# A tuned attention and gMLP kernel: two more Strassen blocks for tokens 512 to 1023, four softmax denominators moved off the matmul engine, and a shorter list of first loads

## The chip, the cores and the metric

The kernel runs on one core of one Trainium2 chip. The metric is the device time of one execution in microseconds (us). The kernel before takes 1762.01 us (median of three executions, 1760.74 to 1764.03).

Names of engines: PE is the matmul engine, PEld its weight loads, DVE the vector engine, ACT the scalar engine, POOL the general engine, SP the engine whose queue issues nearly all DMA here. PSUM is the memory that PE writes its results to. A line such as L507 is a line of the program. The change shifts the program by a few lines, so the same statement is L507 before and L509 after.

## The reference, cut to what matters

```
def A(x, k_cache, v_cache, wq, wo):              # 32 heads of 128, 2048 queries, 2048 keys
    q = (x @ wq) by heads
    p = softmax(q @ k_cache^T * 128 ** -0.5)
    return (p @ v_cache, heads joined) @ wo
def B(x, w_in, w_sp, b_sp, w_out):               # S = 2048 tokens, F = 3584, Fh = 1792
    z = gelu(x @ w_in)
    z1, z2 = z[..., :Fh], layernorm(z[..., Fh:])
    g = einsum('ts,bsf->btf', w_sp, z2) + b_sp   # the spatial gate: mixes tokens
    return (z1 * g) @ w_out                      # the last projection
sa, ca, ga, sb, cb, gb = silu(c) @ w_mod         # six vectors of 1024
x = x + ga * A(layernorm(x) * (1 + ca) + sa, ...)
x = x + gb * B(layernorm(x) * (1 + cb) + sb, ...)
```

All inputs and the output are bf16; x is 2048 tokens by 1024.

## The kernel before

The program is about 1,800 lines. Four of its parts matter here.

**The start.** The first eight tiles of 128 tokens, the vector c and the first pieces of w_mod are loaded on one queue, in this order.

```
for ti in range(8):
    nc.sync.dma_start(xg[ti // 2][:, ti % 2], x_dram[:, ti, :])
    if ti == 1:
        nc.sync.dma_start(c_sb[:], c.rearrange("o (kc p) -> (o kc) p", p=P))
load_wm(2)
load_wm(3)
...                                                             # cut
```

**The attention.** It works through 64 "halves" (one head, 1024 queries each), numbered i = 0 to 63. The softmax denominator of half i - 1 is made during half i, in one of two ways. In halves up to 8 it is made on PE by `finish_here`, eight matmuls with one output column each. Later halves store the partial sums, read them back transposed by a DMA, and reduce them on DVE in `finish_den`. "Halves 5 to 8" are those values of i.

```
def finish_here(i, new_ps=qb_ps):
    dps = new_ps("dps", [P, 8])
    for c_ in range(8):
        nc.tensor.matmul(dps[:, c_:c_ + 1], state[i]["pacc"][:, c_ * P:(c_ + 1) * P],
                         ones_bf[:, 0:1], start=True, stop=True)
    ...                                                         # cut: reciprocal, spread
def finish_den(i):
    ...                                                         # cut
    nc.vector.tensor_reduce(out=den[:], in_=state[i]["pT"][:], op=ALU.add,
                            axis=mybir.AxisListType.X)
    ...                                                         # cut
# per half i and key block kb, near the end of the loop:
        if i > 0:
            work = ({4: lambda i: jobs.append(lambda tag: finish_here(i, tag)),
                     15: load_rec} if i <= 8 else
                    {3: finish_here, 6: load_rec} if final else
                    {0: store_sums, 3: turn_sums, 10: finish_den, 13: load_rec}).get(kb)
            if work:
                work(i - 1)
        if kb == (6 if i <= 9 else 4) and i > 1:
            normalise(i - 2)
```

**Strassen's products.** Where weights and data allow, a 2x2 block product is done with seven products in place of eight; the sums that this takes run on DVE. A `Block` runs its products 1, 2, 6, 7, 5, 3, 4 and empties PSUM through `snap` and `out`, which on DVE take the matmul engine's result and add a second operand (`plus`).

**The end of the program.** The spatial gate has two stages: tokens 0 to 1023, then 1024 to 2047, seven blocks (p = 0 to 6) each. Between them stands the plain last projection of tokens 0 to 1023, in eight tiles of two halves of 14 matmuls. The second stage needs the spatial weights, scaled and summed on DVE (`scale_w`, `w_sums`), and z2, loaded by DMA and normalised on ACT (`norm_z`). After it comes the projection of tokens 1024 to 2047 as four Strassen blocks.

```
def project(ti, between=()):
    ...                                                         # cut
    for j in range(2):
        for f in range(NF):                                     # NF = 14
            nc.tensor.matmul(bo, z1T[0, f // 2][:, f % 2, ti * P:(ti + 1) * P],
                             wout[f // 2][:, f % 2, sl], ...)
        plus(outt[:, sl], bo, x1rs[ti][:, sl])
        work(5 if ti == 2 else 3)()                             # some tasks on DVE
    nc.sync.dma_start(out_dram[:, ti, :], outt[:])

for ti in range(8):
    if ti == 2:
        tasks += scale_w() + w_sums()
    elif ti == 3:
        load_b(1)
        load_z(1, 0, 0)
        load_z(1, 0, 1)
        load_z(1, 1, 0)
        load_z(1, 1, 1)
        load_z(1, 2, 1)
    elif ti == 6:
        norm_z(1, 0, 0)
        norm_z(1, 0, 1)
        norm_z(1, 1, 1)
    project(ti, last + [weights] if not ti else ())
```

The softmax here doesn't subtract the row's maximum and nothing guards it: scores larger than these inputs give would overflow.

Of the kernel before, what the change touches and what calls it, by code (L numbers as in the profile page):

```python
# [9 lines left out]
BF16 = mybir.dt.bfloat16  # L10
# [6 lines left out]
def kernel(  # L17
# [66 lines left out]
    sums_dram = dram.tile([4, P, 1024], BF16)  # L84
    h1_dram = dram.tile([2, P, D], BF16)
    mod_dram = dram.tile([4, D], FP32)
    h2_dram = dram.tile([S, D], FP16)
    rec_dram = dram.tile([2 * H, 1024], FP32)

# [33 lines left out]
    kts[0] = att.tile([P, S], BF16, name="kT", tag="kT", bufs=2)  # L123
    vs[0] = att.tile([P, NKB, DH], BF16, name="v_sb", tag="v_sb", bufs=2)
    nc.scalar.activation(small.tile([P, 1], FP32, name="warm_e")[:], eps_tile[:], ACT.Exp)
    for ti in range(8):
        nc.sync.dma_start(xg[ti // 2][:, ti % 2], x_dram[:, ti, :])
        if ti == 1:
            nc.sync.dma_start(c_sb[:], c.rearrange("o (kc p) -> (o kc) p", p=P))
    load_wm(2)  # L130
    load_wm(3)
    nc.sync.dma_start(wq_g[0][:, :, 0:256], wq_v[:, :, 0:256])
# [646 lines left out]
    for g, (i, kb) in enumerate(steps):  # L779
# [97 lines left out]
            fills(i, kb)  # L877
        if i > 0:
            work = ({4: lambda i: jobs.append(lambda tag: finish_here(i, tag)),
                     15: load_rec} if i <= 8 else  # L880
                    {3: finish_here, 6: load_rec} if final else
                    {0: store_sums, 3: turn_sums, 10: finish_den, 13: load_rec}).get(kb)
            if work:
                work(i - 1)
        if kb == (6 if i <= 9 else 4) and i > 1:
            normalise(i - 2)

    left.__exit__(None, None, None)
# [14 lines left out]
    def scratch(name, shape, dtype=FP32):  # L903
        return scr.tile(shape, dtype, name=name, tag="k2", bufs=11)
# [6 lines left out]
    def after(n, fn):  # L911

        later.append([n, fn])
# [464 lines left out]
    def w_sums():  # L1378

        t = {}  # L1380

        def one(n, u, s):
            if n != 1 and (n, u) not in t:
                t[n, u] = heap.take(f"w_t{n}", [P, 4, 512], FP16)
            t[1, u] = W[0, 1, u]
            a, b = {3: (W[1, 1, u], t[1, u]), 1: (t[1, u], W[0, 0, u]),
                    2: (W[1, 1, u], t[1, u]), 4: (W[1, 0, u], t.get((2, u)))}[n]
            nc.vector.tensor_sub(out=t[n, u][:, s], in0=a[:, s], in1=b[:, s])
            if n == 4 and u == 1:
                for v in range(2):  # L1390
                    wb.update({(1, v): W[0, 0, v], (2, v): W[1, 0, v], (3, v): W[1, 1, v],
                               (4, v): t[4, v], (5, v): t[1, v], (6, v): t[2, v],
                               (7, v): t[3, v]})
        return [lambda n=n, h=h: one(n, h // 2, slice(2 * (h % 2), 2 * (h % 2) + 2))
                for n in (3, 1, 2, 4) for h in range(4)]
# [39 lines left out]
    def work(n=1):  # L1435
        def go():
            for _ in range(n):
                if tasks:
                    tasks.pop(0)()
        return go  # L1440
# [114 lines left out]
        nc.sync.dma_start(x1rs[ti][:], x1_dram[ti])  # L1555

    def project(ti, between=()):
        if ti + 2 < 8:
            load_x1(ti + 2)
        outt = scratch("outt", [P, D], BF16)  # L1560
        for j in range(2):
            sl = slice(j * 512, (j + 1) * 512)
            bo = bank_ps("bo", [P, 512])[:]
            for f in range(NF):
                nc.tensor.matmul(bo, z1T[0, f // 2][:, f % 2, ti * P:(ti + 1) * P],  # L1565
                                 wout[f // 2][:, f % 2, sl], start=(f == 0),
                                 stop=(f == NF - 1), skip_group_check=True)
                if f == NF - 3 and not j:
                    for fn in between:
                        fn()  # L1570
            plus(outt[:, sl], bo, x1rs[ti][:, sl])
            work(5 if ti == 2 else 3)()
        nc.sync.dma_start(out_dram[:, ti, :], outt[:])


# [3 lines left out]
    def unit():  # L1579
        if not units:  # L1580
            t = heap.take("units", [P, 4, 512], FP16)
            units.extend(t[:, k, :] for k in range(4))
        return units.pop(0)

    ps_, pt_ = {}, {}

    def p_sum(p, n):

        z = z1T[1, p]
        a11, a21, a12, a22 = (z[:, k, i * 512:(i + 1) * 512] for k in range(2) for i in range(2))  # L1590
        t = ps_[p, n] = a21 if n == 3 else unit()
        a, b = {1: (a21, a22), 2: (ps_.get((p, 1)), a11), 3: (a11, a21),
                4: (a12, ps_.get((p, 2)))}[n]
        (nc.vector.tensor_add if n == 1 else nc.vector.tensor_sub)(out=t, in0=a, in1=b)

    def wp_sum(p, n):
# [5 lines left out]
                4: (b21, pt_.get((p, 2)))}[n]  # L1602
        nc.vector.tensor_sub(out=t, in0=a, in1=b)

    outts = {}

    def proj_block(m):
        done = {1: 0, 2: 0}

        def operands(n):  # L1610
            sl, ps = slice(m * P, (m + 1) * P), range(NG)
            hi = slice(512 + m * P, 512 + (m + 1) * P)
            a = {1: (0, sl), 2: (1, sl), 7: (0, hi), 4: (1, hi)}.get(n)
            lhs = ([z1T[1, p][:, a[0], a[1]] for p in ps] if a else
                   [ps_[p, {5: 1, 6: 2, 3: 4}[n]][:, sl] for p in ps])
            b = {1: (0, 0), 2: (1, 0), 3: (1, 1)}.get(n)
            rhs = ([wout[p][:, b[0], b[1] * 512:(b[1] + 1) * 512] for p in ps] if b else
                   [pt_[p, {5: 1, 6: 2, 7: 3, 4: 4}[n]] for p in ps])
            return lhs, rhs

        def snap(ps, which):
            t = scratch("snap", [P, 512])[:]
            ti, s0 = ((8 + m, 0), (12 + m, 0), (12 + m, 512))[which - 1]
            plus(t, ps, x1rs[ti][:, s0:s0 + 512])
            return t

        def out(i, j, ps, other):
            ti, sl = 8 + m + 4 * (i - 1), slice((j - 1) * 512, j * 512)
            if not done[i]:
                outts[ti] = scratch("outt", [P, D], BF16)  # L1630
            plus(outts[ti][:, sl], ps, x1rs[ti][:, sl] if other is None else other)
            done[i] += 1
            if done[i] == 2:
                nc.sync.dma_start(out_dram[:, ti, :], outts[ti][:])

        return Block(operands, snap, out)

    def last_block(f, prev):


        def product(n, bank, cols=slice(0, 512), first=True):
# [16 lines left out]
        product(5, a, first=False)  # L1658
        u = f.snap(a, 3)
        product(7, b)  # L1660
        o11, o15 = scratch("outt", [P, D], BF16), scratch("outt", [P, D], BF16)
        done(15, o15, right_, b, u)
        plus(x, b, x)
        c = single_ps("c")[:]
        product(2, c)
        done(11, o11, left_, c, s)
        product(3, a, first=False)
        done(11, o11, right_, a, x1rs[11][:, right_])
        for c0, c1 in ((0, 256), (256, 384), (384, 512)):
            ps = single_ps("d")[:, 0:c1 - c0]  # L1670
            product(4, ps, slice(c0, c1))
            done(15, o15, slice(c0, c1), ps, x[:, c0:c1])

    gates = [[gate_block(c, p) for p in range(NG)] for c in range(2)]
    g = gates[0][0]
# [10 lines left out]
        fn()  # L1686
    for n in (2, 6, 7, 5):
        g.run(n)
    prev = steady(g, gates[0][1:])
    last = [lambda: prev.run(4), lambda: prev.run(3), lambda: heap.give(  # L1690
        *(wb.pop((n, u)) for n in range(1, 8) for u in range(2)))]
# [1 line left out]
    load_x1(1)  # L1693

    def weights():
        for q in WQ:
            load_w(1, *q)

    for ti in range(8):
        if ti == 2:  # L1700
            tasks += scale_w() + w_sums()
        elif ti == 3:
            load_b(1)
            load_z(1, 0, 0)
            load_z(1, 0, 1)
            load_z(1, 1, 0)
            load_z(1, 1, 1)
            load_z(1, 2, 1)
        elif ti == 6:
            norm_z(1, 0, 0)  # L1710
            norm_z(1, 0, 1)
            norm_z(1, 1, 1)
        project(ti, last + [weights] if not ti else ())
    heap.give(*(z1T[0, p] for p in range(NG)))
    for n in (1, 3, 2):
        z_sum(1, 0, n)
    for p in range(NG):
        g = gates[1][p]
        for n, k in ((2, 3), (6, 1), (7, 2), (5, 4)):
            g.on(n, lambda p=p, k=k: wp_sum(p, k))  # L1720
        end = 4 if p + 1 < NG else 3
        g.on(end, lambda p=p: p_sum(p, 1))
        for n, k in ((1, 2), (2, 3), (3, 4)):
            g.on(end, lambda p=p, n=n, k=k: after(n, lambda: p_sum(p, k)))
    prev = steady(None, gates[1])
    projs = [proj_block(m) for m in range(4)]
    for m in range(4):
        for n, k in ((6, 0), (7, 4)):
            if m < 3:
                projs[m].on(n, lambda k=k, m=m: load_x1(9 + m + k))  # L1730
    load_x1(8)
    load_x1(12)
    f = projs[0]
    f.run(1)
    prev.run(4)
    prev.run(3)
    heap.give(*(wb.pop((n, u)) for n in range(1, 8) for u in range(2)))
    for n in (2, 6, 7, 5):
        f.run(n)
    prev = steady(f, projs[1:3])  # L1740
    last_block(projs[3], prev)
    scr_pool.__exit__(None, None, None)
    heap_l.__exit__(None, None, None)
    right.__exit__(None, None, None)
# [28 lines left out]
```

## Time and profile before

| | before |
|---|---|
| device time, median of 3 | 1762.01 us |
| span of the profiled execution | 1759.2 us |
| PE busy | 1734.1 us (99%) |
| PE's share of the chain that ended last | 89% |
| halves 5, 6, 7, 8 | 17.63, 17.47, 19.84, 20.06 us |
| first plain projection matmul to the end of the last matmul | 179.21 us |

A half is counted from one copy of the attention output out of PSUM to the next.

The head of the page of the kernel before: the span, the busy time of each engine, PE's granted clock in 40 slices in tenths of full speed (9 is 90% or more), and the chain by engine.

```profile
span 1759.2 us, 23745 instructions
PE 1734.1 (99%) x8471; PEld 799.8 (45%) x8588; DVE 1489.1 (85%) x2246; ACT 1297.7 (74%) x1529; POOL 30.5 (2%) x39
...
PEclk9999999999999999999999999999999999999999
...
PE 89%; DVE 6%; DMA 2%; ACT 1%; issue 1%; SPq 1%; DVEq 0%; ACTq 0%
```

PE is the limit nearly everywhere. Time falls only if matmuls go away or PE waits less.

The table by windows of the kernel before. Columns: the window from and to, its length, then busy time and number of instructions of PE, PEld, DVE, ACT and POOL, the granted clock, the DMA engines' share, GB/s. The first two windows are 35 us long, the next four are halves 5 to 8, the last is the second half of the plain projection with the start of the second gate stage.

```profile
95.00:130.00 35.00, 34.84 (x174) 16.04 (x176) 31.09 (x45) 32.18 (x32) 4.11 (x3) 1.00 0.67 162
130.00:165.00 35.00, 34.76 (x174) 16.09 (x177) 31.19 (x45) 31.37 (x32) 1.40 (x1) 1.00 0.64 149
116.82:134.45 17.63, 17.52 (x87) 8.03 (x88) 16.89 (x27) 15.98 (x17) 2.79 (x2) 1.00 0.58 137
134.45:151.92 17.47, 17.39 (x88) 8.02 (x88) 16.54 (x25) 16.27 (x17) 0.00 (x0) 1.00 0.80 179
151.92:171.76 19.84, 19.73 (x98) 9.11 (x99) 13.65 (x18) 16.43 (x17) 0.00 (x0) 1.00 0.39 96
171.76:191.82 20.06, 19.89 (x98) 9.10 (x99) 16.05 (x21) 16.38 (x17) 0.00 (x0) 1.00 0.31 79
...
1600.00:1630.00 30.00, 30.00 (x141) 13.62 (x140) 19.90 (x36) 19.77 (x40) 0.00 (x0) 1.00 0.59 167
```

The last line shows PE busy 30.00 of 30.00 us around the place where the second gate stage is to start.

Two places of PE's timeline of the kernel before: a denominator, and another one. Columns: start, busy time of the group (overlap included), engine, line, operation, out<-in, shapes, count.

```profile
140.94 0.34 PE L650 MATMUL dps<-ones_bf,pacc 128*128 128x1 bf16 x8
141.12 0.10 PEld L405 LDWEIGHTS <-wq_t 128*128 128x128 bf16 x1
...
141.36 0.59 PE L507 MATMUL sps<-qT,kT 128*128 128x512 bf16 x2
...
159.05 0.34 PE L650 MATMUL dps<-ones_bf,pacc 128*128 128x1 bf16 x8
159.26 0.59 PE L405 MATMUL qps<-h1T,wq_t 128*128 128x512 bf16 x2
```

At 140.94 eight one-column matmuls start and the next matmul on record starts 0.42 us later. But the second line shows the weights of one more matmul, of L405, loaded at 141.12, and no matmul of L405 follows: its record is missing. At 159.05, where all records are there, the next matmul starts after 0.21 us. The trace of `e1_start` settles it: its attention is that of the kernel before, it has as many matmuls as weight loads on record (8588 each), and at the same place it shows the matmul, 0.20 us after the denominator starts (the lines of its program are one further down):

```profile
141.21 0.34 PE L651 MATMUL dps<-ones_bf,pacc 128*128 128x1 bf16 x8
141.41 0.38 PE L406 MATMUL qps<-h1T,wq_t 128*128 128x512 bf16 x1
```

The queue of SP and the timeline of ACT before the second gate stage, kernel before. Columns: start, busy time of the group (overlap included), engine, line, operation, out<-in, shapes, count. SPq lines are issues of DMA, with the time the issue took on the queue. L1404 loads z2; L1414 normalises it.

```profile
1599.33 0.34 SPq L1573 DMA_DIRECT2D out_dram<-outt  x1
1600.20 0.44 SPq L1404 DMA_DIRECT2D zr<-z_dram  x1
...
1601.31 7.00 SPq L1404 DMA_DIRECT2D zr<-z_dram  x3
```

```profile
1606.68 4.04 ACT L1414 ACTIVATE zr<-zr,z_nm,z_rs 128x256 f16<-128x256 f16 x8 [44.10 <-DMA zr<-z_dram]
1610.63 4.03 ACT L1414 ACTIVATE h_slots<-h_slots,z_nm,z_rs 128x256 f16<-128x256 f16 x8
1614.56 11.89 ACT L1414 ACTIVATE zr<-zr,z_nm,z_rs 128x256 f16<-128x256 f16 x24
```

ACT normalises 40 slices. The bracket is ACT's idle time before the group and what ended it: 44.10 us idle.

### The profile page before, as it was taken

The page shows a single profiled execution, that of the slowest core. Times are in us where ns is not written, and L with a number is a line of the kernel's source. Part 1 is how long each engine was busy: PE and PEld are TensorE (multiplying, and loading weights), DVE is VectorE, ACT ScalarE, POOL GpSimd, SP SyncE. Part 2 cuts the span into 40 slices and gives each one's busy share as a digit, 9 for nine tenths or more (in the row PEclk, how much of TensorE's full clock was granted, in tenths as well). Part 3 has the DMA queues.
Part 4 walks back from the last instruction along what each step waited for, and adds up shares of the span by engine and source line. Part 5 has one row for each costly group of instructions (what it writes and reads, how often), then busy time and mean ns, then how long its engine had stood idle before and what let it go on. Part 6 is the DMA issues. An engine that isn't in the chain of part 4 may idle for free.

```text
span 1759.2 us, 23745 instructions
## 1 busy us (share of the span) xinstructions
PE 1734.1 (99%) x8471; PEld 799.8 (45%) x8588; DVE 1489.1 (85%) x2246; ACT 1297.7 (74%) x1529; POOL 30.5 (2%) x39
## 2 busy tenths in 40 slices
PE   7999999999999999999999999999999999999999
PEld 4444444444444444444444444444444444444444
DVE  6898898898988899998999988986679788775895
ACT  7998889999999999999999999711235666634610
POOL 1010000000000000000000000000000000000000
PEclk9999999999999999999999999999999999999999
DMA  8575366646545633554643475645758544565312
GB/s 252 138 171 135 87 148 154 152 127 161 160 119 137 168 103 102 145 146 134 159 114 102 129 181 134 177 127 158 185 157 211 148 118 118 182 138 148 91 48 72
DMA packets 445335, 247.75 MB, mean 141 GB/s; under 512 B 289312, under 2 KB 406560, under 8 KB 445216
## 3 DMA queue, kind: packets, MB, share of 16 engines
q1 hardware_dynamic: 445216, 246.23, 52.9%
q8 instruction: 67, 1.10, 0.3%
q14 instruction: 52, 0.43, 0.1%
HBM read 144.18 MB, written 52.71 MB: 112 GB/s over the span
## 4 chain that ended last, share of the span: by engine, by line
PE 89%; DVE 6%; DMA 2%; ACT 1%; issue 1%; SPq 1%; DVEq 0%; ACTq 0%
PE ops L775 23%; PE sps L507 22%; PE a L963 16%; PE b L963 9%; PE c L963 4%; PE qa L488 4%; PE qps L405 4%; PE bo L1565 3%; PE qb L488 3%; ACT pt L838 1%; DMA rec_dram<-turned 1%; PE a_11236 L963 1%; DMA wm<-in_w_mod_dram 1%; PE mps L199 0%; DVE sum L1011 0%
## 5 line engine op out<-in xcount | busy, mean ns | idle before, releaser
L838 ACT ACTIVATE pt<-sps 128x1024 bf16<-128x1024 f32 x1008 | 1003.8, 1024 | 81.6 <-PE sps L507 32.4
L507 PE MATMUL sps<-qT,kT 128*128 128x512 bf16 x1986 | 595.5, 379 | 3.2 <-ACT pt L838 2.1
L775 PE MATMUL ops<-pt,v_sb 128*128 128x512 bf16 x2022 | 594.2, 379 | 3.8
L507 PEld LDWEIGHTS <-kT 128*128 128x128 bf16 x2048 | 199.3, 98 | 247.2 <-issue 16.2
L775 PEld LDWEIGHTS <-v_sb 128*128 128x128 bf16 x2048 | 200.1, 98 | 241.9
L1006 ACT ACTIVATE snap<-a 128x512 f32<-128x512 f32 (+1 forms) x111 | 60.6, 565 | 115.1 <-PE a L963 104.8
L854 DVE COPY ou<-ops 128x512 f32<-128x512 f32 x126 | 81.1, 686 | 28.9 <-PE ops L775 26.2
L963 PEld LDWEIGHTS <-h_slots 128*128 128x128 f16 (+1 forms) x689 | 67.3, 98 | 80.3 <-issue 0.9
L405 PE MATMUL qps<-h1T,wq_t 128*128 128x512 bf16 x277 | 93.4, 379 | 0.4
L1011 DVE TENSOR_TENSOR sum<-b,snap 128x512 f32<-128x512 f32 (+1 forms) x76 | 50.1, 660 | 47.3 <-PE b L963 28.0
L1414 ACT ACTIVATE zr<-zr,z_nm,z_rs 128x256 f16<-128x256 f16 x90 | 44.9, 587 | 55.5 <-DMA zr<-z_dram 50.6
L663 DVE TENSOR_TENSOR oT<-ou,rbc 128x1024 bf16<-128x1024 f32 x62 | 75.3, 1215 | 5.7 <-DMA rbc<-rec_dram 5.7
L473 DVE COPY tx<-qa 128x512 f32<-128x512 f32 x66 | 45.4, 688 | 30.3 <-PE qa L488 30.3
L641 DVE TENSOR_REDUCE den<-pT 128x8 f32<-128x1024 bf16 x54 | 64.0, 1185 | 2.8 <-DMA pT<-sums_dram 2.8
L963 PEld LDWEIGHTS <-s_slots 128*128 128x128 f16 (+1 forms) x422 | 41.0, 98 | 51.2 <-DVE s_slots L1336 1.5
L488 PE MATMUL qa<-h1s,wq_t 128*128 128x512 f16 x176 | 63.0, 379 | 0.3
L488 PEld LDWEIGHTS <-wq_t 128*128 128x128 bf16 (+1 forms) x352 | 34.4, 98 | 41.5
L963 PEld LDWEIGHTS <-wq_t 128*128 128x128 f16 (+1 forms) x346 | 33.8, 98 | 39.3 <-DMA wq_t<-oT_dram 0.3
L146 POOL TENSOR_TENSOR rstd<-var,neg_half 128x1 f32<-128x1 f32 x30 | 25.1, 836 | 1301.2 <-DVE var L144 1254.5
L468 DVE TENSOR_TENSOR qT<-qb,tx 128x512 bf16<-128x512 f32 x66 | 45.2, 685 | 0.7
L405 PEld LDWEIGHTS <-wq_t 128*128 128x128 bf16 x288 | 28.0, 98 | 33.2 <-issue 0.6
L1414 ACT ACTIVATE h_slots<-h_slots,z_nm,z_rs 128x256 f16<-128x256 f16 x56 | 28.0, 586 | 19.5 <-DMA h_slots<-z_dram 16.3
(935 smaller groups left out, 2558.5 us busy)
## 6 DMA issues: line engine op xcount, KB each, us to landing
rbc<-rec_dram SPq DMA_DIRECT2D x63, 512.0 KB
v_sb<-in_A_v_cache_dram SPq DMA_DIRECT2D x40, 512.0 KB
oT_dram<-oT SPq DMA_DIRECT2D x62, 256.0 KB
sums_dram<-pacc SPq DMA_DIRECT2D x54, 256.0 KB
wm<-in_w_mod_dram SPq DMA_DIRECT2D x12, 1024.0 KB
wq_t<-in_A_wq_dram SPq DMA_DIRECT2D x7, 1024.0 KB
zr<-z_dram SPq DMA_DIRECT2D x12, 512.0 KB
h_slots<-oT_dram SPq DMA_DIRECT2D x10, 512.0 KB
```

What stands on the lines that cost most here:

```text
L405: nc.tensor.matmul(box["ps"][:], weights[:, dc, hc:hc + DH], src[:, dc, q0:q0 + 512], start=(n == 0), stop=(n == KD - 1))
L488: nc.tensor.matmul(box["b" if m in (2, 7, 4) else "a"][:], *operand(m, dc), start=(m in (1, 2, 7) and dc == 0), stop=(dc == 3), skip_group ...
L507: nc.tensor.matmul(sps[:, j * 512:(j + 1) * 512], kts[h][:, kb * P:(kb + 1) * P], qts[(h, qh)][:, j * 512:(j + 1) * 512], start=True, stop ...
L641: nc.vector.tensor_reduce(out=den[:], in_=state[i]["pT"][:], op=ALU.add, axis=mybir.AxisListType.X)
L663: nc.vector.tensor_mul(out=oT, in0=state[i]["ou"][:], in1=state[i]["rbc"][:])
L775: nc.tensor.matmul(o_ps[j][:], vs[halves[i][0]][:, kb, :], pt_tiles[g][:, j * 512:(j + 1) * 512], start=(kb == 0), stop=(kb == NKB - 1))
L838: nc.scalar.activation(pt_tiles[g], s_tiles.pop(g)[:], ACT.Exp, scale=SCALE, **bias)
L854: nc.vector.tensor_copy(out=ou[:, j * 512:(j + 1) * 512], in_=o_ps[j][:])
L963: nc.tensor.matmul(self.ps[self.BANK[n]], a, b, start=(n in (1, 2, 7) and k == 0), stop=(k == len(lhs) - 1), skip_group_check=True)
L1006: nc.scalar.activation(t, ps, ACT.Copy)
L1414: nc.scalar.activation(z, z, ACT.Identity, scale=z_rs[:, q:q + 1], bias=z_nm[:, q:q + 1])
L1565: nc.tensor.matmul(bo, z1T[0, f // 2][:, f % 2, ti * P:(ti + 1) * P], wout[f // 2][:, f % 2, sl], start=(f == 0), stop=(f == NF - 1), skip ...
```

## The change

Its intent is to take matmuls off PE.

1. *Strassen for tokens 512 to 1023.* Only four plain tiles stay (tokens 0 to 511). The gated data of tokens 512 to 1023 is stored to DRAM (seven stores of 256 KB, `store_zk`), the second gate stage starts 112 matmuls earlier, and at the end two more Strassen blocks of width 256 project the reloaded data.
2. To make room, the *spatial weights* of the second stage are loaded from within the last block of the first stage, scaling and sums run in the four tiles, four last weight sums in the first gate block, and the z2 loads are issued in tiles 1 and 2.
3. *Denominators* of halves 5 to 8 go the DMA and DVE way.
4. *The start*: six loads of one tile become three of two tiles.

```
-    for ti in range(8):
-        nc.sync.dma_start(xg[ti // 2][:, ti % 2], x_dram[:, ti, :])
-        if ti == 1:
-            nc.sync.dma_start(c_sb[:], c.rearrange("o (kc p) -> (o kc) p", p=P))
+    for ti in range(2):
+        nc.sync.dma_start(xg[0][:, ti], x_dram[:, ti, :])
+    nc.sync.dma_start(c_sb[:], c.rearrange("o (kc p) -> (o kc) p", p=P))
+    for j in range(1, 4):
+        nc.sync.dma_start(xg[j], x_dram[:, 2 * j:2 * j + 2, :])
...
-                     15: load_rec} if i <= 8 else
+                     15: load_rec} if i <= 4 else
...
-        if kb == (6 if i <= 9 else 4) and i > 1:
+        if kb == (6 if i <= 5 else 4) and i > 1:
...
-            work(5 if ti == 2 else 3)()
+            work((5, 5, 5, 4, 3, 3, 3, 3)[2 * ti + j])()
...
+    def store_zk():
+        for p in range(NG):
+            nc.sync.dma_start(zk_dram[p], z1T[0, p][:, :, 512:1024])
... (load_zk, z_part, p_sum and proj_block now take a token half c and a width: cut)
+    for n, k in ((1, 0), (7, 1), (5, 2)):
+        gates[0][-1].on(n, lambda k=k: load_w(1, *WQ[k]))
...
-        for q in WQ:
-            load_w(1, *q)
-    for ti in range(8):
-        if ti == 2:
-            tasks += scale_w() + w_sums()
-        elif ti == 3:
-            load_b(1)
+        load_w(1, *WQ[3])
+        sums.extend(w_sums())
+        tasks.extend(scale_w() + sums[:12] + [lambda n=n: z_sum(1, 0, n) for n in (1, 3, 2)])
+    sums = []
+    for ti in range(4):
+        if ti == 1:
             load_z(1, 0, 0)
             load_z(1, 0, 1)
+            store_zk()
+        elif ti == 2:
+            load_b(1)
             load_z(1, 1, 0)
             load_z(1, 1, 1)
             load_z(1, 2, 1)
-        elif ti == 6:
             norm_z(1, 0, 0)
             norm_z(1, 0, 1)
-            norm_z(1, 1, 1)
         project(ti, last + [weights] if not ti else ())
+    while tasks:
+        tasks.pop(0)()
     heap.give(*(z1T[0, p] for p in range(NG)))
-    for n in (1, 3, 2):
-        z_sum(1, 0, n)
+    norm_z(1, 1, 1)
+    for n, fn in zip((6, 6, 7, 7), sums[12:]):
+        gates[1][0].on(n, fn)
...
-    projs = [proj_block(m) for m in range(4)]
+    last_rows = [(1, 0), (1, 1), (1, 2), (1, 3), (0, 0), (0, 1)]
+    projs = [proj_block(*b) for b in last_rows]
...
+    load_zk()
```

## The prediction

> What bounds the kernel now. The page shows PE busy 1734.1 of 1759.2 us at a granted clock of 1.0, and PE is 89% of the chain that ended last. In the table by windows PE is busy 27.90 of 27.90, 24.10 of 24.10 and 80.00 of 80.00 us in the projection of tokens 0 to 1023 and the second gate stage (1576.6 to 1710). About 10 us of PE's idle time lies in the first 15 us. Time is saved by taking matmuls off PE or in the start, and lost where PE waits.
>
> What the change does to PE.
> 1. The timeline shows the projection's 128x512 matmuls starting every 215.7 ns. The Trainium skill, "TensorE: Matmul & The Clock Gate", section "Wait — 56ns, not 53.3ns?", states the same 215.7 ns. Tokens 512 to 1023 take 4 tiles x 2 halves x 14 = 112 matmuls plainly, 2 blocks x 7 products x 7 = 98 by Strassen. 14 fewer: -3.0 us, all on the chain.
> 2. A denominator on TensorE is 8 one-column matmuls; in the timeline at 140.94 the next matmul starts 0.42 us later. Four halves: -1.7 us. In their place come a store, a transposing DMA and a 1.18 us reduction per half on DVE, already busy 31 of every 35 us there. I take 0.4 us back.
> 3. Start: three loads of two rows replace six of one. The queue should issue w_mod about 1.4 us earlier than 4.83 us. But the DMA is at 350 to 380 GB/s from 5 to 25 us, so bytes and not issue set the landing: -0 to -0.5 us.
>
> What may come back as a wait. Four plain tiles stay, from 1576.6 to about 1604.5, where the second gate stage now starts (before: 1628.6). In 1584.1 to 1604.7 DVE was busy 9.3 of 20.6 us. Now it must do 8 outputs (0.69), 16 scalings (about 0.36 in a run), 12 weight sums (0.64), 3 z sums (0.65): about 21 us in 20.6. It just fits, because product 6 of the first gate needs the last z sum only 3.5 us into the stage. Four more sums (2.6 us) go into the first gate, where DVE was at 10.3 of 12.1. I take 0.7 us of PE waiting. The weight loads did not wait for the program: the queue had issued seven of eight by 1580 already, the last at 1583.4 when its slot came free. Two z loads took some 6 us to land; they are now issued about 1588, beside 1.8 MB of stores, and normalised on ACT (4.04 us each) by about 1603.
> At the end, 28 sums of 128x256 (about 0.25 us) go into three projection blocks of 10.6 us; 1.8 MB come back over 30 us. Free.
>
> Sum: -3.0 - 1.7 - 0.2 + 0.4 + 0.7 = -3.8 us: 1758.2 us, range 1755.2 to 1761.6. Within 2% almost surely.
>
> What would show it: 112 matmuls gone from the plain line and 98 more in blocks; four reductions more and 32 one-column matmuls fewer; PE idle below 1 us between 1600 and 1625; start-up within 0.5 us; DVE near 100% from 1584 to 1608.
>
> What would make it wrong: the z or weight loads land late behind the stores and the first gate waits several us; DVE, near full from 115 to 185, holds up PSUM banks by more than the 1.7 us; or the start gains a full microsecond, because DVE idles 0.9 us for the w_mod load at 15.

## The result, and the profile after

| | before | after |
|---|---|---|
| device time, median | 1761.73 us (4 executions, 1760.74 to 1764.03) | 1761.95 us (4 executions, 1761.55 to 1762.51) |
| ratio after to before | | 1.0000, 95% interval 0.9982 to 1.0017 |
| same kernel again, in a later batch, 5 rounds | 1762.88 us | 1761.24 us, ratio 0.9986 (0.9974 to 0.9999) |
| halves 5, 6, 7, 8 | 17.63, 17.47, 19.84, 20.06 us | 18.19, 18.05, 19.64, 19.64 us |
| first plain projection matmul to the end of the last matmul | 179.21 us | 178.39 us |

Ratios here and below are from fast executions alone, and not quite the ratio of the medians that are quoted. An execution is called slow when it is over 1.5% above the fastest of its kernel; none was. Output was correct in all ten experiments. The median is above the predicted range of 1755.2 to 1761.6 us, and 3.75 us above the predicted 1758.2: nearly the whole expected gain is missing.

The head of the page of the kernel after:

```profile
span 1760.4 us, 23835 instructions
PE 1740.1 (99%) x8542; PEld 799.5 (45%) x8542; DVE 1502.9 (85%) x2284; ACT 1298.5 (74%) x1529; POOL 30.5 (2%) x39
```

PE's busy time did not fall, though matmuls are gone: the trace of before lacks the records of 117 matmuls (8471 against 8588 weight loads), that of after lacks none (8542 of each), so the busy times cannot show an effect of 3 us. The weight loads do show what went away: 8588 - 8542 = 46, which is the 14 matmuls of the projection and 32 one-column matmuls of four denominators. For the time the windows are needed. Halves 5 to 8, then the stretch at the start of the second gate stage:

```profile
118.78:136.97 18.19, 17.59 (x81) 7.82 (x80) 17.84 (x27) 15.98 (x17) 2.79 (x2) 1.00 0.67 171
136.97:155.02 18.05, 17.43 (x81) 7.83 (x80) 17.57 (x26) 16.27 (x17) 0.00 (x0) 1.00 0.66 168
155.02:174.66 19.64, 19.64 (x92) 8.88 (x91) 14.74 (x19) 16.43 (x17) 0.00 (x0) 1.00 0.56 133
174.66:194.30 19.64, 19.64 (x92) 8.92 (x91) 17.05 (x22) 16.38 (x17) 0.00 (x0) 1.00 0.38 95
...
1600.00:1630.00 30.00, 28.12 (x130) 12.55 (x129) 25.53 (x48) 23.90 (x49) 0.00 (x0) 1.00 0.70 187
```

Halves 7 and 8 became shorter, by 0.20 and 0.42 us. Halves 5 and 6 became *longer*, by 0.56 and 0.58 us, with DVE now busy 17.84 of 18.19 and 17.57 of 18.05 us. And PE, busy 30.00 of 30.00 us at the start of the second gate stage before, now stands still for 1.88 us of it.

The view of PE's waits says for whom (total, times, longest):

```profile
PE a L965 <- DVE snap L1490: 1.9, 2, 1.4
...
PE sps L509 <- DVE qT L393: 1.0, 2, 0.6
```

Neither line exists in the same view of before. The second is the halves 5 and 6: there the query's copy out of PSUM (`qT`, L393) comes late, and the score matmuls wait 0.40 us at 135.48 and 0.62 us at 153.53. The first is the gate stage. Its chain, followed back through the timelines of PE, DVE, ACT and SP of the kernel after:

```profile
1619.38 1.89 PE L965 MATMUL a<-h_slots 128*128 128x512 f16 x8 [0.45 <-DVE snap L1490]
...
1622.70 1.02 PE L965 MATMUL a<-wq_t 128*128 128x512 f16 x4 [1.44 <-DVE snap L1490]
```

```profile
1616.49 0.69 DVE L1429 TENSOR_TENSOR wq_t<-zr 128x1024 f16<-128x1024 f16 x1 [1.96 <-ACT zr L1418]
...
1618.64 0.68 DVE L1490 SCALAR_TENSOR_TENSOR snap<-a,b_bc 128x512 f32<-128x512 f32 x1
```

```profile
1594.41 4.04 ACT L1418 ACTIVATE zr<-zr,z_nm,z_rs 128x256 f16<-128x256 f16 x8 [30.51 <-DMA zr<-z_dram]
1598.36 4.03 ACT L1418 ACTIVATE h_slots<-h_slots,z_nm,z_rs 128x256 f16<-128x256 f16 x8
1608.49 11.90 ACT L1418 ACTIVATE zr<-zr,z_nm,z_rs 128x256 f16<-128x256 f16 x24 [6.10 <-DMA zr<-z_dram]
```

```profile
1589.84 0.43 SPq L1408 DMA_DIRECT2D zr<-z_dram  x1
...
1591.06 3.71 SPq L1617 DMA_DIRECT2D zk_dram<-z1T  x4
...
1598.06 0.62 SPq L1577 DMA_DIRECT2D out_dram<-outt  x1
...
1599.27 5.64 SPq L1408 DMA_DIRECT2D zr<-z_dram  x3
```

Read from the top: PE waits for a `snap` on DVE. DVE itself was not full: it stood idle for 1.96 us up to 1616.49, waiting for ACT, because the sum of L1429 is of the *second* block's z2. ACT was not slow: it stood idle 6.10 us up to 1608.49, waiting for a DMA. That DMA, the three z2 loads of the second and third block, was issued at 1599.27, behind the two z2 loads of the first block (one of them shown), seven stores of `store_zk` (the first four shown as x4, the others until 1597.2), an output store and two small loads. From there it took until 1608.49 for the first data. The Trainium skill ("Perfetto Trace Analysis", section "DMA Instruction — HWDGE (DVE, Sync)") says that the profiler's window of such a DMA is the issue and leaves the data movement out; here the two really are far apart, 1599.27 and 1608.49.

### The profile page after: what moved, and what is told of

It is laid out like the page before. It is cut to its first block, busy times and chain, and to the rows that moved or that the text cites. A ratio compares the mean times of both kernels' runs of the same rounds, so it can differ in the third digit from the quotient of the medians.

```text
span 1760.4 us, 23835 instructions
## 1 busy us (share of the span) xinstructions
PE 1740.1 (99%) x8542; PEld 799.5 (45%) x8542; DVE 1502.9 (85%) x2284; ACT 1298.5 (74%) x1529; POOL 30.5 (2%) x39
## 4 chain that ended last, share of the span: by engine, by line
PE 88%; DVE 6%; DMA 3%; ACT 2%; issue 1%; SPq 0%; DVEq 0%; ACTq 0%
PE sps L509 23%; PE ops L777 23%; PE a L965 16%; PE b L965 9%; PE c L965 4%; PE qa L490 4%; PE qps L407 4%; PE qb L490 3%; DMA wm<-in_w_mod_dram 1%; ACT pt L840 1%; PE bo L1569 1%; PE a_11218 L965 1%; PE mps L201 1%; DVE sum L1013 0%; DMA zr<-z_dram 0%
## 5 line engine op out<-in xcount | busy, mean ns | idle before, releaser
L509 PE MATMUL sps<-qT,kT 128*128 128x512 bf16 x2048 | 609.2, 379 | 2.4 <-ACT pt L840 1.2
L643 DVE TENSOR_REDUCE den<-pT 128x8 f32<-128x1024 bf16 x58 | 68.7, 1185 | 0.7 <-DMA pT<-sums_dram 0.7
L490 PEld LDWEIGHTS <-tx 128*128 128x128 f16 x264 | 25.8, 98 | 31.2
```

The lines of the kernel that those rows point to most:

```text
L490: nc.tensor.matmul(box["b" if m in (2, 7, 4) else "a"][:], *operand(m, dc), start=(m in (1, 2, 7) and dc == 0), stop=(dc == 3), skip_group ...
L509: nc.tensor.matmul(sps[:, j * 512:(j + 1) * 512], kts[h][:, kb * P:(kb + 1) * P], qts[(h, qh)][:, j * 512:(j + 1) * 512], start=True, stop ...
```

## The experiments

Ten kernels ran, in three batches; each batch has its own executions of the kernel before on the same chip (nine each). Of `e7_dummy` and `e8_storelast` there is one execution each, so only their stretches are used. The milestones of all of them, in us:

| kernel | half 5 | half 6 | half 7 | half 8 | projection to the end |
|---|---|---|---|---|---|
| before | 17.63 | 17.47 | 19.84 | 20.06 | 179.21 |
| after | 18.19 | 18.05 | 19.64 | 19.64 | 178.39 |
| e1_start | 17.63 | 17.47 | 19.84 | 20.06 | 179.40 |
| e2_den | 18.20 | 18.05 | 19.64 | 19.64 | 179.21 |
| e3_tail | 17.63 | 17.47 | 19.84 | 20.07 | 177.71 |
| e4_zfirst | 18.20 | 18.05 | 19.64 | 19.64 | 176.36 |
| e6_best | 17.63 | 17.47 | 19.64 | 19.64 | 176.35 |
| e7_dummy | 18.30 | 18.31 | 19.85 | 20.06 | 179.21 |
| e8_storelast | 18.20 | 18.05 | 19.64 | 19.64 | 176.35 |
| e9_warm | 17.63 | 17.47 | 19.64 | 19.64 | 176.36 |
| e10_mended | 17.64 | 17.46 | 19.64 | 19.65 | 176.37 |
| e11_again | 18.20 | 18.06 | 19.64 | 19.64 | 178.51 |

### The parts alone: e1_start, e2_den, e3_tail

Each takes one part of the change alone, on the kernel before.

```
e1_start: before, with the change's five x loads at the start (hunk "for ti in range(2)") alone
e2_den:   before, with   if i <= 8  ->  if i <= 4   and   kb == (6 if i <= 9 ...)  ->  (6 if i <= 5 ...)
e3_tail:  before, with everything of the change from store_zk to the last block, i.e. not the two above
```

> The kernel before with only the start changed (three loads of two rows). Theory: the two traces show the first ou copy of half 0 at 49.40 us after and 47.44 before, so the reordered loads cost about 2.0 us: w_mod's second load lands near 15.6 instead of 15.07 and TensorE runs its transposes at half rate (0.43 us per 128x512 matmul of zeros, k transposes in 1.9 us) until about 22. Then this run is about +1.9 us over the kernel before, its profile shows 49.4. Rival: the half-rate stretch is an accident of that one execution (phase of the clock window); then the profile shows 47.4 in some run and the timed runs differ by under 0.7 us.

Measured: 1762.58 us against 1762.29 us, ratio 1.0003 (0.9991 to 1.0016). No effect that could be resolved. In its trace half 0 ends at 47.70 us, not at 49.4, so the theory failed: the changed start runs without the loss too. More in step 3 below.

> The kernel before with only the denominators of halves 5 to 8 moved to a DMA and a DVE reduction. Theory from the two traces: halves 5 and 6 (late rows still on DVE) get longer by about 0.57 us each because PE waits for a query copy behind the reduction, halves 7 and 8 get shorter by 0.2 and 0.42: net about +0.5 us, and PE gaps of 0.4 and 0.6 us before an sps matmul released by DVE qT near 133 and 151. Rival (my prediction): DVE has the room and the net is -1.3 us.

Measured: 1760.63 us, ratio 0.9993 (0.9980 to 1.0005), so by whole times not to be told from no effect. In the trace the four halves changed by +0.57, +0.58, -0.20 and -0.42, exactly as in the full change: +0.53 us together. The denominators by themselves *cost* half a microsecond.

> The kernel before with only the tail changed (Strassen projection of tokens 512 to 1023, weight loads moved, 4 plain tiles). Theory: 14 matmuls less is -3.0 us, and about 1.9 us of it is given back as a PE wait in the first gate of the second stage, where z of the second group lands late: net about -1.1 us. Its start is that of the kernel before, so half 0's ou copy is at about 47.4. Rival: the matmuls saved don't show at all (net 0), or the gate wait came only from the later start of that trace (net -3.0).

Measured: 1760.40 us, ratio 0.9992 (0.9980 to 1.0005). From the first plain projection matmul to the end it took 177.71 us, 1.50 less than before; the theory had said 1.1, with a longer wait. One wait of the full change came back, in the timeline of PE:

```profile
1620.20 1.02 PE L964 MATMUL a<-wq_t 128*128 128x512 f16 x4 [1.36 <-DVE snap L1489]
```

So the wait belongs to the tail alone, and 1.50 gained plus 1.36 waited is 2.86 us, close to what the removed matmuls should give (14 matmuls; 3.02 us at 0.2157 us each).

### Whose wait is it: e4_zfirst and e8_storelast

Two theories for the wait at the gate. A: the z2 loads of the second block stand in the queue behind the stores. B: DVE has too much to do, with the four weight sums moved into the first gate block; that was the reason the prediction gave. `e4_zfirst` loads the second block's z2 together with the first's and stores last:

```
@@ e4_zfirst, against the kernel after
             load_z(1, 0, 0)
             load_z(1, 0, 1)
-            store_zk()
-        elif ti == 2:
-            load_b(1)
             load_z(1, 1, 0)
             load_z(1, 1, 1)
+        elif ti == 2:
+            load_b(1)
             load_z(1, 2, 1)
+            store_zk()
```

> The changed kernel with two z loads of the second stage (group 1, both halves) issued with the first two, and the stores of z1T to DRAM after all z loads. Theory: ACT normalised that z only from 1608.5 to 1616.5 because its DMA was issued at 1599.3 behind the stores; DVE waited 1.96 us for it at 1616.5 and PE 1.9 us for DVE. Moved forward, the wait is gone: -1.9 us against the changed kernel, PE idle in the stage under 0.3 us. Rival: DVE has too much work in that stretch (the four last weight sums, 2.6 us); then PE still waits 1 us or more there and the time moves by under 1 us.

Measured: 1759.37 us, ratio 0.9986 (0.9972 to 0.9999). The wait is gone and the stretch is 176.36 us. It changed the order of the loads too, so `e8_storelast` moves the stores and nothing else, by moving one line down:

```
@@ e8_storelast, against the kernel after
             load_z(1, 0, 0)
             load_z(1, 0, 1)
-            store_zk()
         elif ti == 2:
             load_b(1)
             load_z(1, 1, 0)
             load_z(1, 1, 1)
             load_z(1, 2, 1)
+            store_zk()
```

> The changed kernel with only the seven stores of z1T issued after the z loads; the z loads stay where they were in the program. Theory A, the stores hold up the queue and the DMA: the z loads are issued about 1597 in place of 1599.3 (times less the start's shift), land earlier, and PE's wait of 1.9 us in the first gates falls below 0.5. Theory B, their place behind the output store of tile 1, which waits for DVE, is what counts: the wait stays above 1 us.

Measured, one execution: 176.35 us for the stretch. The whole of this trace lies 2.48 us earlier there (first plain projection matmul at 1576.55 against 1579.03). Counted from that matmul, the three loads are issued at 17.33 in place of 20.24 us, and ACT begins with them at 25.75 in place of 29.46 us, 3.7 us sooner (2.9 us of it from the earlier issue, 0.8 us from a shorter way to the first data); ACT's idle time before them, in the bracket, is 2.53 in place of 6.10 us. The queue, ACT and the window of `e8_storelast`:

```profile
1593.88 4.78 SPq L1408 DMA_DIRECT2D zr<-z_dram  x3
1598.70 3.65 SPq L1617 DMA_DIRECT2D zk_dram<-z1T  x4
```

```profile
1602.30 11.90 ACT L1418 ACTIVATE zr<-zr,z_nm,z_rs 128x256 f16<-128x256 f16 x24 [2.53 <-DMA zr<-z_dram]
```

```profile
1600.00:1630.00 30.00, 29.99 (x140) 13.49 (x138) 27.95 (x53) 27.70 (x57) 0.00 (x0) 1.00 0.73 209
```

Theory B falls. DVE keeps all its sums, is busy *more* of this window than in the kernel after (27.95 against 25.53 of 30 us), and PE doesn't wait. The recorded text has another theory B, the output store of tile 1 ahead of the loads; it falls too, for that store is still ahead of them (issued at 1593.01). Only the place of seven stores in the queue differs, so theory A is shown. `e10_mended` moves the same line and has no wait either (176.37 us).

### DVE time alone: e7_dummy

Why do halves 5 and 6 get longer? Theory A: DVE has no room for the reduction. Theory B: it is the traffic of the store and of the transposing DMA, or the later semaphores. `e7_dummy` is the kernel before, denominators still on PE, with one more reduction of the same size (1.21 us in its trace) in halves 5 and 6 whose result nobody reads:

```
@@ e7_dummy, against the kernel before
                 work(i - 1)
+        if i in (5, 6) and kb == 10:
+            spare = small.tile([P, 8], FP32, name="den", tag="den")
+            nc.vector.tensor_reduce(out=spare[:],
+                                    in_=state[i - 1]["pacc"][:].rearrange("p (c k) -> p c k", c=8),
+                                    op=ALU.add, axis=mybir.AxisListType.X)
```

> The kernel before with one extra DVE reduction of 1.18 us, whose result nobody reads, in halves 5 and 6, at the step where the changed kernel has its reduction; denominators stay on TensorE. Theory: DVE's time is what makes PE wait there: PE gaps of 0.4 and 0.6 us before an sps matmul released by DVE qT, and halves 5 and 6 about 1.0 us longer than before each (18.6 and 18.5 in place of 17.63 and 17.47). Rival: the transposing DMA and the queue order make the wait; then the halves stay at 17.63 and 17.47.

Measured, one execution: halves 5 and 6 take 18.30 and 18.31 us, +0.67 and +0.84; halves 7 and 8 are as before. The two windows, and the wait of PE:

```profile
118.77:137.07 18.30, 17.69 (x87) 8.00 (x88) 17.89 (x27) 15.97 (x17) 2.79 (x2) 1.00 0.53 134
137.07:155.38 18.31, 17.55 (x88) 8.01 (x88) 17.61 (x26) 16.25 (x17) 0.00 (x0) 1.00 0.86 185
```

```profile
PE sps L507 <- DVE qT L391: 1.2, 2, 0.7
```

The same wait for the same copy appears with no DMA added at all. DVE time is enough to explain it, and theory B isn't needed. The size is below the microsecond that I had in mind, presumably because part of the reduction still fits into DVE's gaps. The sizes agree with the change: there the same two halves lost 0.56 and 0.58 after a saving of 0.20 each on PE, so the cost on DVE was 0.76 and 0.78 us.

### The best of the parts: e6_best, e9_warm, e10_mended, e11_again

`e6_best` keeps the start of before, takes only the denominators of halves 7 and 8 off PE, and has the tail of `e4_zfirst`:

```
@@ e6_best, against the kernel before: the tail as in e4_zfirst, and
-                     15: load_rec} if i <= 8 else
+                     15: load_rec} if i <= 6 else
-        if kb == (6 if i <= 9 else 4) and i > 1:
+        if kb == (6 if i <= 7 else 4) and i > 1:
```

> The changed kernel with the z loads moved forward, the start of the kernel before, and only the denominators of halves 7 and 8 moved off TensorE. Theory, from the traces so far: halves 5 and 6 are back at 17.63 and 17.47 us, halves 7 and 8 stay at 19.64 and 19.64, the part from the first plain projection matmul to the end is 176.4 us (before 179.2): together -3.5 us against the kernel before in the parts that repeat, plus an unknown of up to 2 us from the start. Rival: the parts interact (the gains don't add): a part is longer than in the run where it stood alone.

Measured: 1758.48 us (1757.14 to 1759.19) against 1761.80 us, ratio 0.9976 (0.9962 to 0.9990). Halves 5 and 6 are back at 17.63 and 17.47 us, halves 7 and 8 keep 19.64 and 19.64, the tail keeps 176.35.

`e9_warm` was about the start. There PE runs some stretches at half rate (below), and I tried to have it up to speed earlier by 15 matmuls of zeros before and after the first small transpose:

```
@@ e9_warm, against e6_best
+    keep_busy(7)
     silu()
+    keep_busy(8)
```

> As e6_best, with 15 more matmuls of zeros on PE before and after the first transpose of c (1 to 7.7 us), where PE is idle. Theory: the start differs by up to 2 us from run to run because PE runs at half rate (0.43 us per matmul of zeros, transposes in 1.9 to 2.1 us per 16) until about 10 to 22 us, by chance; if PE is busy from 1 us on, its transposes at 12 and later are at full rate (1.06 us per 16), half 0's ou copy is at 47.4 or sooner, and the spread of the timed runs is smaller than in e6_best. Rival: the half rate doesn't depend on what PE did before; then nothing changes.

Measured: 1759.77 us, ratio 0.9983 (0.9971 to 0.9996), not faster than `e6_best`. This expectation failed. PE's timeline of `e9_warm`:

```profile
7.96 0.62 PE L293 MATMUL hps<-identity,first_rows 128*128 128x128 bf16 x8 [1.21 <-DVE first_rows L158]
...
16.91 1.06 PE L191 MATMUL zps<-zeros 128*128 128x512 bf16 x2 [0.22 <-issue]
17.77 1.77 PE L293 MATMUL hps<-identity,first_rows 128*128 128x128 bf16 x16
19.38 1.06 PE L313 MATMUL k_ps<-identity,first_rows 128*128 128x128 bf16 x16
```

The warming worked for the first transposes (eight in 0.62 us; 1.04 us without it), but about 16 us PE was at half rate again (two matmuls of 128x512 in 1.06 us, 16 transposes in 1.77 us), then came back (16 in 1.06 us). In narrow windows the column of the granted clock, the third from the right, has this fall (0.52 from 16 to 19 us), which the 40 slices of 44 us at the head of a page cannot show:

```profile
13.00:16.00 3.00, 2.07 (x70) 1.98 (x69) 1.95 (x6) 2.97 (x5) 0.72 (x1) 0.92 1.12 369
16.00:19.00 3.00, 2.69 (x23) 1.54 (x22) 2.61 (x9) 2.26 (x5) 1.01 (x2) 0.52 1.09 383
```

The mean granted clock on record is 0.997 or 0.998 in all five timed executions of `e9_warm`, and 0.998 in two of the five of `e6_best`. Two falls of 3.4 us to half rate make 0.998, so the falls came in every execution with the warming; that this is why it was not faster fits, but was not tested.

`e10_mended` is the kernel after with the two smallest repairs, and `e11_again` the kernel after unedited, side by side on a fresh chip:

```
@@ e10_mended, against the kernel after: the moved line of e8_storelast, and
-                     15: load_rec} if i <= 4 else
+                     15: load_rec} if i <= 6 else
-        if kb == (6 if i <= 5 else 4) and i > 1:
+        if kb == (6 if i <= 7 else 4) and i > 1:
```

> The changed kernel with its two losses mended and nothing else: stores of z1T after the z loads, denominators of halves 5 and 6 back on TensorE; the start stays as changed. Theory: in the parts that repeat it is as e6_best: halves 5 to 8 at 17.63, 17.47, 19.64 and 19.64, from the first plain matmul to the end 176.35 us, so -3.5 us against the kernel before and about -3.2 us against the changed kernel, in the mean of the timed runs within 1 us of that. Rival: the changed start costs a microsecond or more on average; then it is that much slower than e6_best stood (3.3 us under before in medians).

> The changed kernel once more, unedited, for more executions and a second trace. Theory: halves 5 to 8 repeat at 18.19, 18.05, 19.64 and 19.64 us, the wait in the first gates is again 1.4 to 1.9 us, and only the start (half 0's ou copy between 47.2 and 49.4) and single waits move; timed runs on average 0 to 1 us under the kernel before. Rival: the 1.9 us of the start belong to the change; then half 0 is at 49.4 again and the runs average above the kernel before.

Measured: `e10_mended` 1758.70 us (1756.27 to 1760.11) against 1762.88 us, ratio 0.9973 (0.9959 to 0.9986); `e11_again` 1761.24 us, ratio 0.9986 (0.9974 to 0.9999), with the 178.51 us and the long halves 5 and 6 of the first trace of the change. So the change with three lines edited (one moved, two conditions) is faster than the kernel before: by ratio 0.27%, some 4.7 us; its repeated parts account for -2.84 (tail), -0.20 and -0.41 (halves 7 and 8), that is 3.5 us, and the rest lies inside the interval. Against the kernel after, it is 3.2 us shorter in the repeated parts; the whole times of that batch overlap. It is still far inside 2%. Two expectations of `e11_again` were missed: its mean is 2.3 us under that of before, not 0 to 1, and half 0 ended at 49.38 us again, as its rival had said; step 3 below tells why this doesn't point to the changed start.

## Why the prediction was wrong

The prediction expected -3.8 us. The stretches of the trace give -2.86 + 0.52 + 2.04 = -0.30 us, and the first timing found none. Its chances (within 2% almost surely) held, its time and its range did not. Point by point:

**The bound: right.** PE is the limit, and what shortened the kernel in the experiments were matmuls taken away and PE waits removed.

**Step 1, Strassen: right, -3.0 predicted, -2.86 measured.** The plain line went from 224 to 112 matmuls, and without the wait the stretch fell from 179.21 to 176.35 us (e4, e6, e8, e9, e10). The rate of 215.7 ns per 128x512 matmul, which the Trainium skill states in "TensorE: Matmul & The Clock Gate", section "Wait — 56ns, not 53.3ns?", agrees with this trace. The missing 0.16 us sit at the matmul of the second wait, which still starts 0.387 us after the one before in place of 0.216 (e8); what holds it there was not looked into. In halves 7 and 8 after the change PE has no gap, and 19.64 us is 91 such matmuls at 0.2158 us.

**Step 2, the denominators: this step failed, in size and in sign.** The prediction: "Four halves: -1.7 us [...] I take 0.4 us back". Measured: +0.56, +0.58, -0.20, -0.42, together +0.52 us; every kernel with the full change of the denominators (after, e2, e4, e8, e11) repeats each of the four within 0.02 us. Two errors.

- *The saving was read off a place with a missing record.* The 0.42 us at 140.94 hold one more matmul of the query product; only its weight load is on record. A denominator costs PE 0.20 us, not 0.42, as the other places (0.21 at 159.05, 0.20 in `e1_start`) and half 7 (19.84 to 19.64) show. In half 8 a further 0.22 us was gained. Before, two query matmuls there took 0.81 in place of 0.59 us; that they waited for the PSUM bank of the denominator is argued, not shown.
- *The room on DVE was averaged over too wide a window.* "Already busy 31 of every 35 us" is true of two windows of 35 us, but halves 5 and 6 alone had 0.74 and 0.93 us free, and the reduction takes 1.18 us. The Trainium skill says of the vector engine that a reduction has no faster mode ("VectorE: DVE Perf Modes", section "The perf-mode tier table") while an operation on two bf16 tensors has one; this trace agrees, 1.18 us to reduce a 128x1024 bf16 tile and 0.69 us for a sum of two f16 tiles of that size (16 bit as well). The reduction pushes the copy of the query out of PSUM back, for which PE waits. e7 shows that DVE time alone does that. In halves 7 and 8, with 13.65 of 19.84 and 16.05 of 20.06 us busy, the same reduction was free. This kernel has "multiple regimes, where the most-contended engine changes over time", as the Trainium skill puts it ("Perfetto Trace Analysis", section "Optimization Strategy"): in halves 5 and 6 DVE is as near its limit as PE.

The prediction did name this danger, "DVE, near full from 115 to 185, holds up PSUM banks by more than the 1.7 us", but priced it at 0.4 us; it was 0.76 + 0.78 = 1.54 us.

**The wait at the gate: this term failed too, in size and in cause.** The prediction: "I take 0.7 us of PE waiting", for a DVE that had to take "four more sums (2.6 us)". Measured: 178.39 - 176.35 = 2.04 us (2.16 in the second trace of the change, 1.36 for the tail alone). DVE was not the cause: it idled 1.96 us just then, and in e8 it did all of those sums in time. The prediction's own sign, DVE near 100% from 1584 to 1608, did not come either: it was busy 20.23 of those 24.00 us. The cause is the queue's order. The prediction followed only the first two z2 loads and called the 1.8 MB of stores something "beside" them. The first two did come in time, normalised by 1602.4 ("by about 1603"). The next three, for the second and third block, stood behind the seven stores, and ACT could begin with them 3.7 us later than without (e8). "The z or weight loads land late behind the stores" does stand in the list of what would make the prediction wrong; the order of the queue in the diff would have told me that it must happen, had I written down the issue time of every load behind the stores and when its first reader needs it.

**Step 3, the start: no error that could be measured.** -0.2 us predicted, with 0 to -0.5 as its range. The loads are issued earlier (w_mod at 3.54 us in place of 4.83) but are used no earlier (the first matmul on w_mod at 14.30 us in place of 13.99). That bytes set the time, as predicted, fits the 368 to 390 GB/s of both traces from 7 to 22 us. I took the trace of the change at first for a loss of 1.96 us, since its half 0 ended at 49.40 in place of 47.44 us. The parts of that in PE's timeline are stretches at half rate. The kernel before, then the kernel after:

```profile
19.15 1.06 PE L312 MATMUL k_ps<-identity,first_rows 128*128 128x128 bf16 x16
```

```profile
20.08 1.91 PE L314 MATMUL k_ps<-identity,first_rows 128*128 128x128 bf16 x16
```

But over all twelve traces this comes and goes with either start. The end of half 0 stands at 47.24, 47.70, 48.59, 49.38, 49.40 and 50.32 us with the changed start, at 47.41, 47.44, 47.55, 49.16, 49.17 and 49.38 us with the old one. The Trainium skill, "TensorE: Matmul & The Clock Gate", section "What's actually happening", says that the array starts at half rate, that a free-running window releases it, and that the moment varies from run to run. The traces agree. The clock records in them, which the clock column averages, change in steps of 3.41 us (stretches of 3.41, 10.24 and 13.65 us), and the first release came at any time from 12.4 to 22.2 us, at 5.25 us in e9.

The same records sort the twelve numbers. Where PE was released between 13.9 and 14.9 us and stayed at full rate, half 0 ended at 47.24 and 47.70 us with the changed start and at 47.41, 47.44 and 47.55 us with the old one. Where it was released earlier and fell back to half rate for 3.41 us at about 16 and once more at about 30 us, half 0 ended at 49.38 and 50.32 us with the changed start and at 49.16, 49.17 and 49.38 us with the old one. The other two are `e4_zfirst`, with one fall at 28.4 us (48.59), and the trace of the change, released only at 22.23 us (49.40). So like compared with like, no loss from the changed start is seen; in the group without falls the two starts differ by under 0.5 us. Why an early release is followed by a fall is left open.

**What stays open.** Some later halves are up to 0.9 us longer in some traces, whatever the kernel (half 47 took 16.83 to 17.66 us); in the trace of before DVE waits 1.64 us there for a DMA of the denominators, which I didn't pursue. The start is a part of the 1.4 us by which executions differ: of the 27 executions of before, the 8 with a mean granted clock of 0.998 took 1763.8 us on average, the 15 with 1.000 took 1761.9 us. That such chance is also why the first timing of the change gives a ratio of 1.0000 and the second 0.9986 is a guess. The -0.3 us of the stretches is a ratio of 0.9998, which lies within both intervals (0.9982 to 1.0017 and 0.9974 to 0.9999).

## What to carry to other kernels

Before work is moved to another engine, look up that engine's free time in each single stretch where the work lands, not in a window that spans several; 0.8 us free do not hold a reduction of 1.2 us, whatever the average says. When stores are put into a queue that also carries loads, write down the issue time of every load behind them and of its first reader, not only of the next load; stores nobody waits for belong last. And read a small cost from several places of a trace, checking that the weight loads and the matmuls match, before multiplying it. Before a difference at the start is put down to an edit, compare traces with the same course of the granted clock, in windows of a few us.

## What the Trainium skill lacked or had wrong

- "TensorE: Matmul & The Clock Gate", "What's actually happening": that all matmuls after the first 3.4 us run at full rate ("everything after runs at 2.4 GHz") did not hold here. In `e9_warm` PE was at full rate at 7.96 us (eight transposes in 0.62 us) and at half rate again at 16.91 us (16 transposes in 1.77 against 1.06 us), with no idle stretch longer than 1.46 us in between. The page itself describes falls later on: the section "HAM oscillation — how this bites in real kernels" has DMA waits of over 3.4 us as the cause, which is not the case here; the section after it has frequent short idling, which may be.
- No page that I read says that a trace's clock records can begin only with the first release, so that the granted-clock column stays at 1.00 while matmuls run at half rate before it: in the trace of before they begin at 13.89 us, and at 7.75 us eight transposes take 1.04 us with the column at 1.00. Later falls are in the column (0.52 in `e9_warm`).
- "Perfetto Trace Analysis" warns that a DMA's window is its issue, but gives no figure for the time to the landing behind other traffic: three z2 loads issued at 1599.27 behind 1.8 MB of stores let their reader start at 1608.49, 9.2 us later; issued at 1593.88 ahead of the stores (e8), 8.4 us later. The loads are 0.8 us slower; the rest of the 3.7 us was the place in the queue.
- No page that I read warns that matmul records can be missing from a trace while their weight loads are there (8471 matmuls against 8588 weight loads in the trace of before, 8588 of each in that of `e1_start`), which is how 0.20 us was read as 0.42.
